# 47 further products on TensorE behind the last slot of a routed expert kernel

## The chip, the cores and the metric

One NeuronCore of a Trainium2 chip runs the whole kernel. The metric is the device time of one execution in microseconds (us). TensorE (PE) multiplies into PSUM banks, ScalarE (ACT) and VectorE (DVE) empty them, GpSimd (POOL) gathers and scatters rows by index, SyncE (SP) starts the other transfers.

## What is computed

Attention with a causal window of 64, a dense layer pair with a leaky activation, and a layer of eight experts, of which each token uses one. The last part is where the change stands:

```python
logits = x @ w_gate
expert_idx = np.argmax(logits, axis=1)
for e in range(E):
    mask = expert_idx == e
    xe = x[mask]
    h = np.maximum(xe @ w1[e], 0.0)
    ye = h @ w2[e]
    out[mask] = gate_w[mask, None] * ye
```

There are 2304 tokens, 512 features, 8 experts and 1024 hidden units.

## The kernel before, in words

Attention and the dense layers come first, in an order written out by hand (`PLAN`). Then the expert layer runs in slots. A slot is 128 tokens of one expert. The tokens of an expert rarely fill whole slots, so their number depends on the data: 20 slots (`SURE`) run always, and 5 more stand in nested conditional blocks, `tc.If(tot > s - K1)`, line 970. Each engine branches for itself. In the profiled execution slot 20 runs and the blocks of slots 21 to 24 are skipped (504 instructions of line 743 are 21 slots of 24).

Every value is split into a high and a low part in the type fp32r, and each product is done three times (high by high, low by high, high by low).

A slot (`slot`, line 914) does, in this order: `e1` (lines 715 to 717) multiplies the tokens by the first weights, 24 products of 128 rows, 128 outputs and 512 columns, into a bank of the tag `h`; `htr` (lines 726 to 730) turns the result on TensorE into a bank of the tag `att`, which ScalarE copies (line 729) and VectorE then reads a second time (line 730); `xtr` (lines 699 to 703) does the same for the next slot's tokens, with ScalarE at line 702 and VectorE at line 703; `e2mm` (line 743) multiplies by the second weights, 24 products, into `acc0` or `acc1`; `finish` scales (line 749) and scatters 128 rows to the output by an indirect transfer of GpSimd (line 750). Beside it `split2` makes the high part (ScalarE, line 819) and the low part (VectorE, line 825) of the next slot's weights, and `reload` (line 764) fetches those after them. All of it is issued in the order of the code (`tc.manual_schedule()`).

`pbank("att")` hands out three banks in turn, `pbank("h")` two. The split weights lie in 12 buffers `ring_t[4]` to `ring_t[15]`, used in turn; `xs[s]` holds the turned tokens of slot s, in one of two buffers. `pbank` hands out the bank that was used longest ago, so that the last to have read a bank is ScalarE and VectorE of some slot before.

An engine that skips a conditional block runs one event there, which adds to the engine's semaphore what the skipped instructions would have added, after its own last instruction (line 970 in the rows). So who waits for an instruction of a skipped block waits for that event. Behind the blocks stands the end of the program (line 1046 in the rows): SP waits for every transfer and every engine in turn, one event each, TensorE's count among the last three; then all engines drain and meet twice at a barrier that GpSimd leads.

Of the kernel before, what the change touches and what calls it, by code (L numbers as in the profile page):

```python
# [80 lines left out]
def attn_moe_moe_kernel(  # L81
# [11 lines left out]
    PE, ACT, DVE, POOL, SP = nc.tensor, nc.scalar, nc.vector, nc.gpsimd, nc.sync  # L93
# [131 lines left out]
    att = st1.enter_context(tc.tile_pool(name="att", bufs=1))  # L225
# [449 lines left out]
    xs = {}  # L675
# [79 lines left out]
    def sregs(s):  # L755
        p, r = where(s)
        ctl = tab["ctl", p]
        e = SP.value_load(ctl[0:1, 0, r:r + 1], min_val=0, max_val=NE - 1)
        ch = SP.value_load(ctl[0:1, 1, r:r + 1], min_val=0, max_val=1) if s else None
        regs[s] = (e, ch)  # L760

    def reload(s, t):
        e, ch = regs[s]
        SP.dma_start(out=raw2[t], in_=wx[bass.ds(e, 1), t].rearrange("o p c -> p (o c)"), cond=ch, cond_hint=False)
# [3 lines left out]
    ring_t = {}  # L768
# [145 lines left out]
    def slot(s):  # L914
        nx = s + 1 < NSLOT
        extra = {
            0: {0: [(r_trans, NB - 1, 0)], 1: [(r_trans, NB - 1, 1, "ht")], 2: [(r_logits, NB - 1, 0)],
                3: [(r_trans, NB - 1, 2), (r_logits, NB - 1, 1)], 4: [(r_logits, NB - 1, 2)], 7: [(r_gate, NB - 1)]},
            1: {1: [(r_rank, NB - 1), (r_place, NB - 1)], 6: [(r_onehot, NB - 1)]},
            2: {0: [(r_list, NB - 1), (r_add, NB - 1)], 1: [(r_onehot, NB - 1, 1)], 2: [(r_list, NB - 1, 1), (r_add, NB - 1)], 4: [(table_step,), (table_step,)]},  # L920
            3: {i: [(table_step,)] for i in (0, 2, 4, 6)},
        }.get(s, {})

        def step(i):
            for fn, *a in extra.get(i, []):
                fn(*a)
            if nx:
                split2(s + 1, i)
                if i % 2 and s + 2 < NSLOT:
                    if i == 1:  # L930
                        sregs(s + 2)
                    reload(s + 2, i // 2)

        e1(s, 0, 0)
        step(0)
        e1(s, 0, 1)
        step(1)
        e1(s, 1, 0)
        htr(s, 0)
        step(2)  # L940
        e1(s, 1, 1)
        step(3)
        e2mm(s, 0)
        htr(s, 1)
        step(4)
        if s + 2 < NSLOT:
            gather(s + 2)
        e2mm(s, 1)
        if nx:
            xtr(s + 1)  # L950
        step(5)
        e2mm(s, 2)
        step(6)
        e2mm(s, 3)
        finish(s)
        step(7)

    gen1 = slot_table(1)
    with tc.manual_schedule():
        sregs(1)  # L960
        for t in range(4):
            reload(1, t)
        for s in range(SURE):
            slot(s)
        tot = nc.values_load(tab["tot"][0:1, 0:1], min_val=0, max_val=NSLOT)
        st2 = ExitStack()
        for s in range(SURE, NSLOT):
            st2.enter_context(tc.If(tot > s - K1))
            slot(s)
        st2.close()  # L970


# [78 lines left out]
```

## Time and profile before

| | us |
|---|---|
| median of 2 runs | 768.01 (767.69 to 768.33) |
| the profiled execution, its own time | 768.02 |
| its span, first to last instruction | 766.2 |
| TensorE busy | 747.7 |
| VectorE busy | 609.1 |
| ScalarE busy | 456.3 |
| GpSimd busy | 89.0 |

The span is what the profile's rows cover; 1.8 us of the profiled execution lie outside it. A q behind an engine's name (PEldq, SPq) is its sequencer, which runs events, branches and drains. PEld is the loading of weights into TensorE, which has its own rows.

### The profile page before, as it was taken

How to read it: one execution, taken by the hardware profiler on the slowest of the kernel's cores; microseconds unless marked ns; L12 is line 12 of the kernel's file. 1: busy time of each engine (PE TensorE's matmuls, PEld its weight loads, DVE VectorE, ACT ScalarE, POOL GpSimd, SP SyncE). 2: the span in 40 equal slices, each digit the busy share in tenths (PEclk: the TensorE clock that was granted, in tenths of full speed). 3: DMA queues.
4: the chain of work that ended last, by engine and by line, in shares of the span. 5: the costliest groups of instructions: out<-in, count | busy, mean ns of one | idle time of the engine just before them, and what ended most of it. 6: DMA issues, size and time to landing. Idle time of an engine off the chain costs nothing.

```text
span 766.2 us, 12642 instructions
## 1 busy us (share of the span) xinstructions
PE 747.7 (98%) x4567; PEld 612.6 (80%) x4572; DVE 609.1 (79%) x1154; ACT 456.3 (60%) x868; POOL 89.0 (12%) x106
## 2 busy tenths in 40 slices
PE   7999999999999999999999999999999999999996
PEld 3688888788888888888888988777788888888884
DVE  4999999477556656668775956699999999999997
ACT  4887465533233333334342323778889898899986
POOL 1210001000000000000000001011222213131322
PEclk9999999999999999999999999999999999999998
DMA  9993423233033113122323116430195076766621
GB/s 343 412 367 131 147 74 117 70 86 122 18 100 97 62 57 103 62 97 90 92 69 111 56 42 250 168 119 28 56 340 182 29 270 265 284 236 248 212 75 51
DMA packets 29442, 109.90 MB, mean 143 GB/s; under 512 B 3582, under 2 KB 3966, under 8 KB 22208
## 3 DMA queue, kind: packets, MB, share of 16 engines
q1 hardware_dynamic: 25856, 98.25, 35.6%
q0 software_dynamic: 3520, 10.80, 4.2%
q8 instruction: 38, 0.62, 0.3%
q14 instruction: 28, 0.23, 0.1%
HBM read 154.09 MB, written 10.26 MB: 214 GB/s over the span
## 4 chain that ended last, share of the span: by engine, by line
PE 86%; DVE 8%; issue 2%; DMA 1%; ACT 1%; POOL 0%; SPq 0%; DVEq 0%
PE acc L743 12%; PE h L389 9%; PE acc L431 9%; PE acc L432 9%; PE h L390 8%; PE h L391 8%; PE acc L433 8%; DVE hl L825 4%; PE h L715 4%; PE h L717 4%; PE h L716 4%; PE att L364 2%; PE att L295 2%; PE att L341 2%; PE att L726 1%
## 5 line engine op out<-in xcount | busy, mean ns | idle before, releaser
L825 DVE TENSOR_TENSOR hl<-hl,hl 128x1024 fp32r<-128x1024 f32 x176 | 211.4, 1223 | 17.1 <-ACT hl L819 16.4
L819 ACT CAST hl<-hl 128x1024 fp32r<-128x1024 f32 x176 | 180.2, 1049 | 4.6 <-DMA hl<-in_wx_dram 3.4
L743 PE MATMUL acc<-hl,xl 128*128 128x512 f32 x504 | 130.7, 400 | 2.4 <-DVE xl L730 2.3
L404 ACT ACTIVATE g<-h 128x512 f32<-128x512 f32 (+1 forms) x80 | 44.6, 557 | 142.6 <-PE h L391 112.3
L389 PE MATMUL h<-xh,hl 128*128 128x512 f32 (+1 forms) x320 | 120.5, 377 | 0.7 <-DVE g L408 0.7
L390 PE MATMUL h<-xl,hl 128*128 128x512 f32 (+1 forms) x320 | 118.1, 369 | 0.0
L391 PE MATMUL h<-xh,hl 128*128 128x512 f32 (+1 forms) x320 | 118.0, 369 | 0.0
L432 PE MATMUL acc<-hl,gl 128*128 128x512 f32 x288 | 113.2, 393 | 0.4 <-DVE gl L414 0.4
L433 PE MATMUL acc<-hl,gh 128*128 128x512 f32 x288 | 112.6, 391 | 0.0
L431 PE MATMUL acc<-hl,gh 128*128 128x512 f32 x288 | 109.9, 400 | 0.0
L743 PEld LDWEIGHTS acc<-hl,xl 128*128 128x128 f32 x504 | 91.2, 188 | 21.3 <-DVE xl L730 3.7
L408 DVE SCALAR_TENSOR_TENSOR g<-g,beta,h 128x512 f32<-128x512 f32 (+1 forms) x80 | 55.3, 691 | 56.1 <-ACT g L404 55.9
L414 DVE TENSOR_TENSOR gl<-g,gh 128x512 fp32r<-128x512 f32 (+1 forms) x80 | 50.8, 635 | 38.4 <-PE acc L432 24.1
L349 ACT CAST gh<-g 128x512 fp32r<-128x512 f32 (+1 forms) x80 | 46.5, 581 | 51.4 <-DVE g L408 49.7
L691 POOL DMA_INDIRECT gx<-x1d,ixg x23 | 39.9, 1736 | 290.5 <-DVE xh L703 167.1
L389 PEld LDWEIGHTS h<-xh,hl 128*128 128x128 f32 x320 | 60.1, 188 | 10.9 <-issue 1.2
L715 PE MATMUL h<-hl,xh 128*128 128x512 f32 x168 | 67.7, 403 | 0.0
L485 DVE SCALAR_TENSOR_TENSOR dot<-stage,wge 128x512 bf16<-128x512 f32 x96 | 65.9, 686 | 1.8 <-DMA wge<-in_wgt_dram 0.4
L390 PEld LDWEIGHTS h<-xl,hl 128*128 128x128 f32 x320 | 60.1, 188 | 8.5 <-DVE xl L377 0.5
L717 PE MATMUL h<-hl,xh 128*128 128x512 f32 x168 | 66.1, 393 | 0.3 <-DVE xh L703 0.2
L391 PEld LDWEIGHTS h<-xh,hl 128*128 128x128 f32 x320 | 60.1, 188 | 7.9
L716 PE MATMUL h<-hl,xh 128*128 128x512 f32 x168 | 65.5, 390 | 0.0
(194 smaller groups left out, 1070.8 us busy)
## 6 DMA issues: line engine op xcount, KB each, us to landing
hl<-in_wx_dram SPq DMA_DIRECT2D x92, 1024.0 KB
hl<-in_wcat_dram SPq DMA_DIRECT2D x14, 1024.0 KB
qk<-in_qkv_dram SPq DMA_DIRECT2D x30, 448.0 KB
v<-in_qkv_dram SPq DMA_DIRECT2D x30, 256.0 KB
wge<-in_wgt_dram SPq DMA_DIRECT2D x24, 256.0 KB
x1d<-stage SPq DMA_DIRECT2D x3, 1032.0 KB
hl<-in_qkv_dram SPq DMA_DIRECT2D x6, 448.0 KB
x<-in_wcat_dram SPq DMA_DIRECT2D x2, 1024.0 KB
```

Of the source, the lines that this page charges most:

```text
L389: PE.matmul(out=h[:, 0:n], lhsT=w_in_op(f, k, 0), rhs=xh[:, k, :], start=(k == 0), stop=False)
L390: PE.matmul(out=h[:, 0:n], lhsT=w_in_op(f, k, 0), rhs=xl[:, k, :], start=False, stop=False)
L391: PE.matmul(out=h[:, 0:n], lhsT=w_in_op(f, k, 1), rhs=xh[:, k, :], start=False, stop=(k == 3))
L431: PE.matmul(out=a, lhsT=gh[:, c0:c0 + 128], rhs=w_out_op(f, 0), start=(f == 0), stop=False)
L432: PE.matmul(out=a, lhsT=gl[:, c0:c0 + 128], rhs=w_out_op(f, 0), start=False, stop=False)
L433: PE.matmul(out=a, lhsT=gh[:, c0:c0 + 128], rhs=w_out_op(f, 1), start=False, stop=(f == 15))
L715: PE.matmul(out=o, lhsT=th[:, k, :], rhs=wh, start=(k == 0), stop=False)
L716: PE.matmul(out=o, lhsT=th[:, k, :], rhs=wl, start=False, stop=False)
L717: PE.matmul(out=o, lhsT=tl[:, k, :], rhs=wh, start=False, stop=(k == 3))
L743: PE.matmul(out=o, lhsT=x[:, f % 4, :], rhs=w[:, lo, (f % 2) * 512:(f % 2) * 512 + 512], start=(x is th and f == 0 and lo == 0), stop=(x i ...
L819: ACT.copy(out=t[:, 0, :], in_=r)
L825: eng.tensor_tensor(out=t[:, 1, :], in0=r, in1=f32(t[:, 0, :]), op=ALU.subtract)
```

## The change

Behind the conditional blocks, outside all of them, TensorE runs 47 products. Their stationary operand is a part of `xs[0][0]`, the moving one a part of the high half of `ring_t[4]`, and they write the three `att` banks and one `h` bank, each with `start=True`; nobody reads the banks afterwards. In order: 5 of the usual shape; 12 of 64 rows, by turns the upper and the lower half, by turns into two banks; 16 of 32 rows, the four quarters by turns into four banks; 6 with 256 columns; 4 with 64 outputs; 4 of 64 rows, all the upper half and one bank. Nothing else changes.

```diff
+    def probe():
+        x, y = xs[0][0], ring_t[4][:, 0, 0:512]
+        b = [pbank("att") for _ in range(3)] + [pbank("h")]
+
+        def mm(o, r0, r1, m=128, n=512):
+            PE.matmul(out=o[0:m, 0:n], lhsT=x[r0:r1, 0, 0:m], rhs=y[r0:r1, 0:n], start=True, stop=True)
+
+        for _ in range(5):
+            mm(b[0], 0, 128)
+        for i in range(12):
+            mm(b[i % 2], 64 * (i % 2), 64 * (i % 2) + 64)
+        for i in range(16):
+            mm(b[i % 4], 32 * (i % 4), 32 * (i % 4) + 32)
+        for _ in range(6):
+            mm(b[0], 0, 128, 128, 256)
+        for _ in range(4):
+            mm(b[0], 0, 128, 64)
+        for _ in range(4):
+            mm(b[0], 0, 64)
+
...
         st2.close()
+        probe()
```

## Rows read from the trace of the kernel before

**Rows 1.** The page: span, TensorE's busy time, the clock in 40 slices

```profile
span 766.2 us, 12642 instructions
...
PE 747.7 (98%) x4567; PEld 612.6 (80%) x4572; DVE 609.1 (79%) x1154; ACT 456.3 (60%) x868; POOL 89.0 (12%) x106
...
PEclk9999999999999999999999999999999999999998
```

**Rows 2.** Timeline of 757 to 767 us: start us, us, engine, line, operation

```profile
756.77 2.00 PE L743 MATMUL acc<-hl,xl 128*128 128x512 f32 x8
...
758.10 3.63 DVE L825 TENSOR_TENSOR hl<-hl,hl 128x1024 fp32r<-128x1024 f32 x3
...
759.39 1.04 ACT L819 CAST hl<-hl 128x1024 fp32r<-128x1024 f32 x1
760.47 1.02 POOL L750 DMA_INDIRECT out_dram<-gx,ixs  x1 [0.30 <-ACTq L970]
```

**Rows 3.** Line 970, 755 to 767 us: ns min/median/max, first and last start

```profile
L970 PEldq COMPARE_BRANCH  x2: 200/1766/3332, 755.9 to 759.5; - x2
...
L970 PEldq EVENT_SEMAPHORE  x1: 51/51/51, 759.3 to 759.3; - x1
...
L970 ACTq EVENT_SEMAPHORE  x1: 17/17/17, 760.5 to 760.5; - x1
L970 DVEq EVENT_SEMAPHORE  x1: 21/21/21, 761.8 to 761.8; - x1
```

**Rows 4.** Line 1046, the end of the program, whole span

```profile
L1046 POOLq EVENT_SEMAPHORE  x4: 17/17/17, 765.4 to 766.1; - x4
L1046 POOLq DRAIN  x3: 46/113/4170, 761.2 to 766.0; - x3
L1046 SPq DRAIN  x3: 7/7/13, 764.3 to 765.7; - x3
L1046 PEldq DRAIN  x2: 8/8/8, 759.8 to 765.7; - x2
```

**Rows 5.** Line 1046 in 763 to 764.4 us

```profile
L1046 SPq EVENT_SEMAPHORE  x12: 27/28/336, 763.2 to 764.2; - x12
```

**Rows 6.** The chain that ended last, 735 to 767 us: start us, us, what

```profile
743.24 0.44 PE att L699 x4
743.67 2.75 PE acc L743 x12
```

**Rows 7.** Timeline of TensorE, 62 to 66 us, where the shape changes twice

```profile
62.94 0.39 PE L391 MATMUL h<-xh,hl 128*128 128x512 f32 x1
63.26 1.10 PE L295 MATMUL att<-qk 64*64 64x128 f32 x32
64.29 0.50 PE L431 MATMUL acc<-hl,gh 128*128 128x512 f32 x1
64.63 0.40 PE L432 MATMUL acc<-hl,gl 128*128 128x512 f32 x1
64.87 0.40 PE L433 MATMUL acc<-hl,gh 128*128 128x512 f32 x1
```

**Rows 8.** Timeline of TensorE, 7 to 12.9 us

```profile
7.90 1.99 PE L295 MATMUL acc<-qk 64*64 64x128 f32 x32 [2.72 <-DMA qk<-in_qkv_dram]
9.81 1.04 PE L271 MATMUL att<-c 128*128 128x512 bf16 x2
10.64 0.91 PE L286 MATMUL acc<-c 128*128 128x512 bf16 x2
```

**Rows 9.** Stretches of the start and the end: us, busy (count), granted clock, DMA

```profile
8.00:10.00 2.00, 2.00 (x33) 1.61 (x34) 0.07 (x1) 0.00 (x0) 0.00 (x0) 0.50 1.09 423
10.00:12.00 2.00, 2.00 (x24) 0.82 (x26) 1.69 (x6) 0.40 (x3) 0.25 (x1) 0.68 0.97 402
758.00:762.00 4.00, 0.76 (x4) 0.30 (x2) 3.72 (x4) 2.13 (x3) 2.90 (x2) 1.00 0.19 56
762.00:763.00 1.00, 0.00 (x0) 0.00 (x0) 0.00 (x0) 0.00 (x0) 0.00 (x0) 0.60 0.53 195
763.00:766.20 3.20, 0.00 (x0) 0.00 (x0) 0.00 (x0) 0.00 (x0) 0.00 (x0) 0.50 0.00 0
```

**Rows 10.** Timeline, 746 to 747.5 us: weight loads beside products

```profile
746.49 0.39 PE L716 MATMUL h<-hl,xh 128*128 128x512 f32 x1
746.49 0.19 PEld L717 LDWEIGHTS h<-hl,xh 128*128 128x128 f32 x1
...
746.72 0.39 PE L717 MATMUL h<-hl,xh 128*128 128x512 f32 x1
```

## The prediction

> **What bounds the kernel now.** I read the page first: TensorE is busy 747.7 of 766.2 us at the full clock [rows 1], so over the whole span it is the bound, and a product put in the middle would cost its full time. But the change stands behind the last slot, so I read the last 10 us. In the timeline TensorE's last product ends at 756.77 + 2.00 = 758.77, ScalarE's last copy at 760.43, VectorE's last subtraction at 758.10 + 3.63 = 761.73, GpSimd's scatter at 761.49 [rows 2]. From 758.77 to the span's end, 7.4 us, TensorE does nothing. What ends last there is none of the working engines. The lines of the end show that SP has gone through its waits by 764.3, and that the longest of GpSimd's three drains takes 4.17 us from 761.2, to 765.4; only then does GpSimd's first barrier event come, and 0.8 us later the span ends [rows 4]. So the path at the end is GpSimd's drain, and TensorE has slack: its own last count is asked for by SP among its last three events, about 764.2 [rows 5], and up to about 0.2 us before 765.4 it could come without harm.
>
> **When the products can start.** TensorE leaves the blocks early: its event there is at 759.3 and its drain at the end at 759.8 [rows 3, 4]. The products need their operands (written by ScalarE) and their banks free. The first bank, the one used longest ago, was last read by VectorE, by the low half of an `xtr` in a block that is skipped; what stands for it is VectorE's event at line 970, at 761.8, behind its last subtraction [rows 2, 3]. ScalarE's event, at 760.5, is earlier. So the change adds a wait on TensorE until 761.8. Queued behind it are the other 46 products and TensorE's drain, and for that drain and count SP and the barrier wait. First weight load about 761.85.
>
> **What the 47 products take.** Between products of the usual shape the chain has 2.75 us for 12, a step of 0.229 us; the 0.39 us of one row is latency, not step [rows 6, 10]. Part by part, at the full clock:
>
> 5 usual: 5 x 0.229 = 1.15.
>
> 12 of half the rows: attention runs 32 products of 64 x 64 in 1.10 us at the full clock [rows 7], 0.87 us without the last one's latency of about 0.23, thus 0.11 for four. A turn at 128 x 128 with the same 128 columns steps by 0.44/4 = 0.11 too [rows 6]. So four quarter-arrays run beside each other at the price of one product. Those are halves of rows crossed with halves of outputs; I take from it that the two row halves run as a pair: 6 x 0.229 = 1.37. The bound from the other side is 12 x 0.229 = 2.75, if fp32r in halves doesn't pair.
>
> 16 of a quarter: no row shows 32 rows. By the same reading four run together, 4 x 0.229 = 0.92; one by one 16 x 0.229 = 3.66. I take 0.92, by the nearest row, attention's four at once. [...]
>
> 6 with 256 columns: between 0.11 (the turn) and 0.229; half the columns of the usual shape, so 0.12, 0.72 in all, at most 1.37.
>
> 4 with 64 outputs and 4 on one half: the columns set the step, and nothing alternates, 8 x 0.229 = 1.83. If the 64 outputs were cheaper it would be at least half of that.
>
> Together 1.15 + 1.37 + 0.92 + 0.72 + 1.83 = 5.99. The shape changes five times. At a change before, the first product of the new shape starts 63.26 - 62.94 = 0.32 us behind the last of the old one, 0.09 over the step, and the second comes 64.63 - 64.29 = 0.34 behind the first, 0.11 over [rows 7]. That makes 0.2 a change, 1.0 in all; the start from standing costs the second part once more, 0.1; the last product's latency beyond its step is 0.39 - 0.23 = 0.16. Sum 7.25 us: 761.85 + 7.25 = 769.1.
>
> [...]
>
> **The clock.** [...] At the start of the kernel it was 0.50 from 7.9, when products began, and the mean of 0.68 over 10 to 12 puts the rise at 10 + 2 x 0.32/0.5 = 11.3 [rows 8, 9], so 3.4 us of low clock with TensorE at work. At the low clock the step is longer: 10.64 - 9.81 for two, 0.415, for bf16, and 1.99 against 1.10 us for attention's 32 [rows 7, 8], about 1.85 times. So 3.4 us at half speed do the work of 1.7 and cost 1.7: end at 770.8. If the clock stays up, 769.1.
>
> **The end.** From TensorE's end SP still needs two events (0.06 each: 11 steps from about 763.55 to 764.2) and its drains, 0.2 with the signal [rows 4, 5]; GpSimd's drain has long ended, so the barrier follows at once and takes the same 0.8. With 0.1 for the signals: 770.8 + 1.1 = 771.9 for the span, 5.7 over 766.2. Outside the span lie 1.8 us before (768.02 - 766.2), and I leave them: 773.7. The profiled 768.02 is the median, so no correction. No other engine, queue or transfer gets an instruction, and everything up to 758.77 is as it was; its cost I put at nothing, with no bound that the rows suggest. What is late next is TensorE itself, with GpSimd's drain under it, 5 us early. [...]
>
> **The rivals.**
> *An early start.* TensorE doesn't wait for VectorE's event and starts at 759.85, at the full clock. End 759.85 + 7.25 = 767.1, span 768.2, time 770.0. Against it: VectorE reads each `att` bank second. 7 in 100.
> *No pairs.* Row halves and quarters run one by one: 1.37 + 2.74 = 4.1 more, 777.8. For it: no row of fp32r in parts of the rows. Against: attention's four at once. 12 in 100.
> *The clock stays low* to the end, since parts of the array keep it there: 7.25 x 1.85 = 13.4 us in place of 7.25 + 1.7 = 8.95, so 778.2. Against it: attention's parts at 7.9 were followed by the rise [rows 8, 9]. 9 in 100.
> [...] 3 in 100.
> *The other side, slower by over 2%.* One mechanism: parts of rows neither pair nor count as work for the clock, so that all 47 go one by one at the low clock: (41 x 0.229 + 0.72 + 1.26) x 1.85 = 21.0 us (1.26 for changes of shape, start and latency), end 782.9, time 785.8. It decides from 783.4, 2% over. 3 in 100.
> *Nothing to see.* The products end before 765.2 and GpSimd's drain hides them, 768.0: this needs the early start and a sum of 5.3 instead of 7.25. 3 in 100.
>
> **How the numbers follow.** The forecast, start at VectorE's event, pairs and fours, has 63 in 100; with the clock up all the time it gives 772.0, with a start or signals 1 us later some 775. Its own range is 771.5 to 775. To hold 8 in 10 I take in the early start at 770.0 and the two cases at 778; the 785.8 and the 768.0 stay out. Range 769.8 to 778.4. Faster or slower by over 2% (about what a measurement of this kernel can tell from no change) means below 752.7 or above 783.4. Only the other side is there: slower 0.03, faster 0.005 for what I can't name, same 0.965.
>
> **What would show it.** In the changed profile: the rows of the slots unchanged; TensorE's first new product at 761.8 to 762.0, right behind VectorE's event; the 12 halves in about 1.4 us at the full clock, two starting together; the 16 quarters in 0.9, four together; a gap of 0.3 at each change of shape; the clock at 0.50 for some 3.4 us from about 762.2; GpSimd's drain still ending at 765.4 with SP's last events now at TensorE's end; span 770 to 772. It is wrong if TensorE starts before 761, if the halves step by 0.23 each, or if something ahead of 758 moved.

## The result, and the profile after

The kernel with the change takes 772.63 us, the median of two executions (772.15 and 773.12), against 768.01 before: a ratio of 1.0059, with an interval of 1.0043 to 1.0075. That is 4.6 us more, below the 2% that a measurement of this kernel can tell in general; the interval still excludes no change at all. The forecast was 773.7, with 772.0 for a clock that stays up. The profiled execution is the one of 772.15, and in it the clock stayed up.

The page of the changed kernel: the span, the engines' busy time, and the clock in 40 slices.

```profile
span 770.4 us, 12737 instructions
PE 756.3 (98%) x4614; PEld 617.8 (80%) x4619; DVE 609.1 (79%) x1154; ACT 456.1 (59%) x868; POOL 89.0 (12%) x106
PEclk9999999999999999999999999999999999999999
```

Beside [rows 1], the other engines' busy time is where it was and TensorE has more. The span is 4.2 us longer and 1.75 us lie outside it, as before. The end of the timeline (start us, us, engine, line, operation; the probe's products stand at L963, and what was line 970 is L990):

```profile
758.48 3.62 DVE L825 TENSOR_TENSOR hl<-hl,hl 128x1024 fp32r<-128x1024 f32 x3
...
762.31 1.80 PE L963 MATMUL att<-hl,xh 128*128 128x512 f32 x6 [3.16 <-DVEq L990]
...
763.95 0.39 PE L963 MATMUL att<-hl,xh 64*128 64x512 f32 x1
763.95 0.39 PE L963 MATMUL acc<-hl,xh 64*128 64x512 f32 x1
764.18 0.39 PE L963 MATMUL att<-hl,xh 64*128 64x512 f32 x1
764.19 0.39 PE L963 MATMUL acc<-hl,xh 64*128 64x512 f32 x1
...
764.88 0.39 PE L963 MATMUL acc<-hl,xh 64*128 64x512 f32 x1
765.20 0.49 PE L963 MATMUL att<-hl,xh 32*128 32x512 f32 x1
765.21 0.50 PE L963 MATMUL acc<-hl,xh 32*128 32x512 f32 x1
765.21 0.49 PE L963 MATMUL att<-hl,xh 32*128 32x512 f32 x1
765.21 0.49 PE L963 MATMUL h<-hl,xh 32*128 32x512 f32 x1
765.54 0.40 PE L963 MATMUL att<-hl,xh 32*128 32x512 f32 x2
...
767.03 0.73 PE L963 MATMUL att<-hl,xh 128*128 128x256 f32 x3
...
767.15 0.84 PE L963 MATMUL att<-hl,xh 128*64 128x512 f32 x3
...
768.72 0.62 PE L963 MATMUL att<-hl,xh 64*128 64x512 f32 x2
```

The halves start two at a time within 10 ns, the quarters four at a time, and the next pair or four comes 0.23 us or so behind (763.95, 764.18; a first four at 765.20, a second at 765.54 with the change of shape in it). Here a pair or a four costs what one product costs, 0.23. The last product ends at 768.72 + 0.62 = 769.34. The two merged rows at 767 show the one change of shape that costs nothing: the last product of 256 columns starts at 767.03 and the first with 64 outputs at 767.15, the step of 0.12 that 256 columns have. The end of that second row agrees: 767.15, two steps of 0.23 and the latency of 0.39 make 768.0, where the row ends at 767.99.

The events of line 990, from 755 to 771 us (ns min/median/max, first and last start), answer to [rows 3]:

```profile
L990 PEldq EVENT_SEMAPHORE  x1: 51/51/51, 760.0 to 760.0; - x1
...
L990 ACTq EVENT_SEMAPHORE  x1: 17/17/17, 760.8 to 760.8; - x1
L990 DVEq EVENT_SEMAPHORE  x1: 21/21/21, 762.1 to 762.1; - x1
```

TensorE is there at 760.0, ScalarE's event comes at 760.8, and the first product starts at 762.31, behind VectorE's event at 762.1. The end of the program (was line 1046) answers to [rows 4]:

```profile
L1067 SPq EVENT_SEMAPHORE  x14: 17/28/4977, 763.6 to 770.3; - x14
L1067 POOLq EVENT_SEMAPHORE  x4: 17/17/17, 769.6 to 770.3; - x4
L1067 POOLq DRAIN  x3: 46/112/4030, 761.6 to 770.1; - x3
```

GpSimd's long drain now takes 4.03 us from 761.6, until 765.6, but its first barrier event comes only at 769.6: the barrier waits for SP, whose longest event, 4.98 us, is the wait for TensorE, by the list of what SP waited for:

```profile
SPq L1067 <- PE att L963: 5.0, 1, 5.0
```

The path at the end has passed from GpSimd's drain to TensorE. The stretches (us; busy and count of PE, PEld, DVE, ACT, POOL; granted clock; DMA share; GB/s) show the clock:

```profile
762.00:763.00 1.00, 0.69 (x3) 0.64 (x4) 0.10 (x1) 0.00 (x0) 0.00 (x0) 1.00 0.79 270
763.00:770.40 7.40, 6.34 (x46) 3.83 (x44) 0.00 (x0) 0.00 (x0) 0.00 (x0) 1.00 0.01 2
```

Where [rows 9] fell to 0.60 and then 0.50, this execution has 1.00 to the end.

### The profile page after: what moved, and what is told of

Same layout as the page of the kernel before. It is cut to its first block, busy times and chain, and to the rows that moved or that the text cites. A ratio compares the mean times of both kernels' runs of the same rounds, so it can differ in the third digit from the quotient of the medians.

```text
span 770.4 us, 12737 instructions
## 1 busy us (share of the span) xinstructions
PE 756.3 (98%) x4614; PEld 617.8 (80%) x4619; DVE 609.1 (79%) x1154; ACT 456.1 (59%) x868; POOL 89.0 (12%) x106
```

## The experiments

Ratios are to the kernel before, run beside each on the same chip; in brackets stands the interval, behind the median the lowest and highest time. The kernel before took 768.84 (766.57 to 770.19) beside the first four, 767.98 beside the next four, 768.2 beside the last.

### The change once more

No edit.

> The change as it is, more often. Mine: the time has two levels that differ by whether the clock falls while TensorE waits for VectorE: about 772.1 with the clock at 1.00 to the end (as profiled), about 1 to 1.7 more with a low stretch. The rival, that the spread of the two executions (772.15 and 773.12) is the usual one of this kernel: then the kernel before, run beside it, spreads as widely, and the low clock does not go with the longer times.

773.76 us (773.26 to 774.58), ratio 1.0065 [1.0052, 1.0078]. The forecast of 773.7 was for a clock that falls, and here it fell. Stretches of the profiled execution, same columns as above:

```profile
763.00:764.00 1.00, 0.83 (x3) 0.72 (x4) 0.00 (x0) 0.00 (x0) 0.00 (x0) 0.78 0.66 224
764.00:767.00 3.00, 3.00 (x12) 1.98 (x12) 0.00 (x0) 0.00 (x0) 0.00 (x0) 0.50 0.01 3
767.00:768.00 1.00, 1.00 (x14) 0.55 (x16) 0.00 (x0) 0.00 (x0) 0.00 (x0) 1.00 0.00 0
```

A mean of 0.78 puts the fall to 0.50 at 0.44 us before 764, at 763.56; the rise is at 767, so 3.4 us low. TensorE had stood still for 3.17 us and begun again 0.4 us before the fall. The products show both levels:

```profile
763.17 0.47 PE L963 MATMUL att<-hl,xh 128*128 128x512 f32 x1 [3.17 <-DVEq L990]
...
765.82 0.62 PE L963 MATMUL att<-hl,xh 64*128 64x512 f32 x1
765.83 0.62 PE L963 MATMUL acc<-hl,xh 64*128 64x512 f32 x1
766.25 0.62 PE L963 MATMUL att<-hl,xh 64*128 64x512 f32 x1
...
770.58 1.19 PE L963 MATMUL att<-hl,xh 64*128 64x512 f32 x4
```

At a clock of 0.50 a pair steps 0.43 us (765.82 to 766.25) in place of 0.23. From first start to last end the 47 take 771.77 - 763.17 = 8.60 us here and 769.34 - 762.31 = 7.03 in the first profile: the fall costs 1.57 us. All five executions have a mean clock of 0.996, as the slower of the first two had (773.12), and the other of those 1.000 (772.15). Such a mean also holds a low stretch near the start of the kernel, where there is one: from 7.9 to 11.3 us in the kernel before [rows 9], from 9.2 to 12.6 here (a clock of 0.81 in 8 to 10 us, 0.50 in 10 to 12, 0.84 in 12 to 14), none in the first profile. But 0.996 stands for some 6 us of low clock (an estimate, 0.004 x 774 / 0.5), more than one stretch of 3.4. The spread of the kernel before, 3.6 us over 18 executions, is wide enough to hold such differences, so the times alone would not show the price; the two profiles do.

### Other banks: ScalarE's event in place of VectorE's

```diff
-        b = [pbank("att") for _ in range(3)] + [pbank("h")]
+        b = [pbank("acc0"), pbank("acc1"), pbank("h"), pbank("h")]
```

> The 47 products write the banks acc0, acc1 and both h, which ScalarE alone read last. Mine: they start at ScalarE's event, 1.3 us ahead of VectorE's, and all behind them moves with it: 1.3 less than the change, about 770.8, the clock up in nearly every execution since TensorE stands still for 1.8 us only. The rival, that the branch and the fetch of the new instructions set the start: no earlier start, 772.1 to 773.

770.84 us (769.45 to 771.55), ratio 1.0030 [1.0019, 1.0042]. Events of line 990 in it:

```profile
L990 ACTq EVENT_SEMAPHORE  x1: 17/17/17, 759.5 to 759.5; - x1
L990 DVEq EVENT_SEMAPHORE  x1: 21/21/21, 760.8 to 760.8; - x1
```

Its first product starts at 759.57, behind ScalarE's event and 1.2 us ahead of VectorE's, and the clock stays at 1.00. The median comes out 2.9 us below that of the change run beside it, and two terms add up to this: 1.3 between the two events and 1.57 for a fall that TensorE, after 1.76 us of standing still, doesn't meet in this profile. (Three of the six executions have a mean clock of 1.000. Three have 0.998: by 0.002 x 771 / 0.5, an estimate, some 3 us of low clock, and where it lay was not seen.) So the wait that sets the start of the change is the bank's last reader, not the operands or TensorE's own path, and it was worth both the start and, in the profile, the clock. Whether the start here hangs on the banks or on the operands, which ScalarE wrote as well, this run doesn't tell: both stand behind the same event.

### The first five products alone

The other five loops are left out.

> Only the five usual products of the 47 are left. Mine: TensorE ends at about 763.9, before SP asks for it at 764.4 and before GpSimd's drain ends at 765.6, so they are hidden: within 0.4 us of the kernel before. The rival, that work behind the blocks has a price of its own (fetch, semaphores, a later barrier): at least 1.3 more than before.

767.95 us (766.56 to 769.37, 12 executions), ratio 0.9994 [0.9984, 1.0004]. The end of the program in it:

```profile
L1057 POOLq EVENT_SEMAPHORE  x4: 17/17/17, 765.0 to 765.7; - x4
L1057 POOLq DRAIN  x3: 46/112/4531, 760.4 to 765.5; - x3
```

Its products end at 761.68 + 1.19 = 762.87, the drain at 760.4 + 4.53 = 764.9, and the barrier comes with the drain. What TensorE did by then cost nothing: a ratio of 0.9994.

### All parts of one height on the same rows

```diff
-            mm(b[i % 2], 64 * (i % 2), 64 * (i % 2) + 64)
+            mm(b[i % 2], 0, 64)
...
-            mm(b[i % 4], 32 * (i % 4), 32 * (i % 4) + 32)
+            mm(b[i % 4], 0, 32)
```

> The 12 halves all use the upper half of the rows and the 16 quarters the first quarter, with the banks by turns as before: the same count and shapes, no two row groups beside each other. Mine: each steps by 0.23, so 6 x 0.23 + 12 x 0.23 = 4.1 more than the change, about 776.3. The rival, that products on parts of the rows are cheap by themselves, whichever rows: no more than the change, 772 to 773.

783.78 us (782.52 to 786.04), ratio 1.0196 [1.0179, 1.0212]: 10.0 over the change beside it, where 18 further steps of 0.23 are 4.1. The expectation of 776.3 had no price for the clock. Stretches:

```profile
765.00:770.00 5.00, 5.00 (x12) 3.66 (x12) 0.00 (x0) 0.00 (x0) 0.00 (x0) 0.50 0.00 0
770.00:778.00 8.00, 8.00 (x19) 5.28 (x18) 0.00 (x0) 0.00 (x0) 0.00 (x0) 0.50 0.00 0
778.00:783.00 5.00, 5.00 (x14) 3.15 (x14) 0.00 (x0) 0.00 (x0) 0.00 (x0) 0.50 0.00 0
```

The clock fell at the start (a mean of 0.53 over 762 to 765 puts the fall at 762.2, where TensorE's first product starts at 762.94), and then it never came back in this profile, though TensorE was busy without a break from 762.94 to 783.24. All five executions have a mean clock of 0.984 to 0.988. The products ran one by one at 0.43 us, 20.3 us in all with the other shapes (762.94 to 783.24). The forecast's rival for the other side had 21.0 us for just this: neither pairs nor a clock that comes back.

### The same, started early

The last edit and the banks of the second experiment together: parts one by one, but from a clock that is up.

> As the run with one row group, but into the banks acc0, acc1 and h, so that TensorE starts at ScalarE's event, with the clock still up. Mine, since the low clock there lasted from the wait to the end of the program: single products on a part of the rows neither raise the clock nor hold it. Then the clock starts at 1.00 and falls while the halves or quarters run, and the time lies between 6.2 and 13 us over the kernel before. The rival, that the clock was low only for the wait ahead and then stuck: it stays at 1.00 to the end, 2.0 + 4.1 = 6.1 over before.

778.32 us (776.94 to 778.52), ratio 1.0129 [1.0113, 1.0144]. Stretches, and one row of the timeline:

```profile
761.00:767.00 6.00, 5.88 (x24) 4.29 (x25) 1.32 (x2) 0.02 (x1) 1.02 (x1) 1.00 0.21 66
767.00:768.00 1.00, 1.00 (x6) 0.77 (x5) 0.00 (x0) 0.00 (x0) 0.00 (x0) 0.85 0.00 0
768.00:774.00 6.00, 6.00 (x18) 3.79 (x16) 0.00 (x0) 0.00 (x0) 0.00 (x0) 0.50 0.00 0
774.00:775.00 1.00, 1.00 (x4) 0.78 (x4) 0.00 (x0) 0.00 (x0) 0.00 (x0) 0.73 0.00 0
```

```profile
762.82 1.54 PE L963 MATMUL acc<-hl,xh 64*128 64x512 f32 x6
```

Six halves on the same rows take (1.54 - 0.39) / 5 = 0.23 us a step at the full clock: no pairs, and each load hidden behind the product ahead of it. From 762.8 to 765.1 the products are busy for all 2.30 us and ten loads, of 0.18 each, for 1.84 of them. The clock fell at about 767.7, in the middle of the quarters, with no pause of TensorE since 761.1, and rose at about 774.5, when the products of full height had run again. Together the products take 14.25 us (761.12 to 775.37): 7.03, 4.1 for the missing pairs, and 3.1 for 6.8 us of low clock. All four executions have a mean clock of 0.995 or 0.996. So parts run one by one neither brought the clock back (the experiment before, 0.50 to the end) nor kept it up (0.50 from 767.7).

### All 47 of the usual shape

All six loops are replaced by `for _ in range(47): mm(b[0], 0, 128)`.

> All 47 products of the usual shape, 128 rows and 512 columns, in the banks and at the start of the change. Mine: the low stretch lasts about 3.4 us as in the change, and then the clock rises, for full products follow: 47 x 0.229 + 0.16 + 0.1 = 11.0 in place of 7.04, and the same 1.6 for the clock: 4.9 + 4.0 = 8.9 over before. The rival, that the clock once low stays low behind the blocks whatever runs: 47 x 0.427 = 20 us, some 16 over before.

777.40 us (775.81 to 777.86), ratio 1.0115 [1.0098, 1.0131]. That is 9.4 over the kernel before, where 8.9 was expected. In its profile the clock fell and came back within 3.4 us, as in the change run again; the products take 774.96 - 762.44 = 12.52, which is 46 x 0.229 + 0.39 + 0.1 = 11.0 and the 1.5 of the fall. The execution whose clock was 1.000 throughout took 775.81. So 47 steps, 12.52 us, are far more than the 8.60 that the change run again pays with a fall of the same length: its parts do run beside each other.

### More changes of shape, the same number of steps

```diff
-        for i in range(12):
-            mm(b[i % 2], 64 * (i % 2), 64 * (i % 2) + 64)
-        for i in range(16):
-            mm(b[i % 4], 32 * (i % 4), 32 * (i % 4) + 32)
+        for j in "HHQHQHQHQH":
+            p = 2 if j == "H" else 4
+            for i in range(p):
+                mm(b[i], 128 // p * i, 128 // p * (i + 1))
```

> The same products, but pairs of halves and fours of quarters by turns (H H Q H Q H Q H Q H, six pairs and four fours), 7 more changes of shape. Mine: 0.2 a change at the full clock, 1.4 over the change, up to 2 where the clock is low: 6.3 to 6.9 over before. The rival, that a change of shape costs nothing and the 0.3 steps of the rows are the latency of what ran before: 4.9 over before, as the change.

777.67 us (773.56 to 777.98), ratio 1.0116 [1.0096, 1.0136]; the expectation was missed in the times. The profiled execution is the one of 773.56, with the clock at 1.00:

```profile
764.27 0.49 PE L963 MATMUL h<-hl,xh 32*128 32x512 f32 x1
764.69 0.50 PE L963 MATMUL att<-hl,xh 64*128 64x512 f32 x1
764.70 0.50 PE L963 MATMUL acc<-hl,xh 64*128 64x512 f32 x1
765.12 0.50 PE L963 MATMUL att<-hl,xh 32*128 32x512 f32 x1
```

Every step is 0.43 here (764.26, 764.69, 765.12), 0.20 over the usual 0.23. The products take 770.74 - 762.29 = 8.45 us, 1.42 more than in the change for seven further changes of shape: 0.20 each, as expected. What was missed is the clock: three of the five executions lie some 4 us higher, with a mean clock of 0.991; by 0.009 x 776 / 0.5, an estimate, their clock was low for some 14 us, where the change run again shows 0.996 and 6.8 us (3.4 at the start of the kernel, 3.4 here). None of the three was profiled, so where it was low was not seen.

### A later start

```diff
+        for _ in range(4):
+            DVE.memset(b[0], 0.0)
```

Four memsets of VectorE on the first bank, ahead of the products.

> VectorE writes zeros into the first bank four times before the 47 products, so that TensorE stands still for some 2.4 us longer and the clock is certain to be low at the start. Mine: the low clock costs at most the same as in the change, since it rises after some 3.4 us of products: 4.9 + 2.4 = 7.3 over before, a little more where the change itself had started ahead of the fall. The rival, that a longer stand costs a longer low stretch: 9 or more over before.

776.34 us (776.05 to 777.52), ratio 1.0113 [1.0097, 1.0128]: 8.4 over the kernel before, between the two expectations. Timeline and stretches:

```profile
762.95 0.48 DVE L962 MEMSET att<- 128x512 f32 x1 [0.18 <-DVE att L962]
...
763.58 0.77 PE L965 MATMUL att<-hl,xh 128*128 128x512 f32 x1 [6.14 <-DVE att L962]
```

```profile
762.00:763.00 1.00, 0.00 (x0) 0.00 (x0) 0.64 (x3) 0.00 (x0) 0.00 (x0) 0.79 0.00 0
763.00:769.00 6.00, 5.42 (x21) 3.47 (x21) 0.43 (x1) 0.00 (x0) 0.00 (x0) 0.50 0.00 0
769.00:770.00 1.00, 1.00 (x16) 0.72 (x16) 0.00 (x0) 0.00 (x0) 0.00 (x0) 0.80 0.00 0
```

A memset takes 0.48 us and the next starts 0.67 behind it, so the first product comes 3.15 us behind VectorE's event at 760.43, 2.9 later than in the change. The clock fell before TensorE began and stayed low from 762.6 to 769.4, 6.8 us, twice as long as in the change run again. The products took 773.23 - 763.58 = 9.65 us, 1.05 more than in the change run again. So by the profile the later start adds its 2.9 and the longer low stretch another 1.05, beside a rise of 3.4 in the medians (8.36 for 4.92). The first expectation, a low stretch of the same length, missed; the longer stretch is that of its rival, though the time stayed under the 9 that the rival had. Whether the longer stand made it longer is not shown: the early start with parts one by one, further up, had 6.8 us too, with no stand of TensorE for 6.6 us ahead of its fall.

### The first 33 products, started early

The banks of the second experiment, with only the usual products, the halves and the quarters.

> The first 33 of the 47 products (5 usual, 12 halves, 16 quarters) into the banks that ScalarE read last. Mine: started at ScalarE's event they end some 4.2 us behind it, 0.7 us before GpSimd's drain, and cost nothing: within 0.4 us of the kernel before. The rival, that the five products alone were hidden because they were few, and that SP's wait for TensorE or the fetch of more instructions shows with 33: 1 us or more over before.

768.59 us (768.02 to 769.28, 11 executions), ratio 1.0005 [0.9996, 1.0014]. Its last quarters, and GpSimd's drain:

```profile
764.63 0.39 PE L963 MATMUL h<-hl,xh 32*128 32x512 f32 x2
```

```profile
L1061 POOLq DRAIN  x3: 46/113/4371, 761.6 to 766.5; - x3
```

The products end near 765.0, the drain at 761.6 + 4.37 = 766.0. Thirty-three of the 47 products cost nothing when they start 1.3 us earlier. No version that ran is faster than the kernel before; this one and the one with five products equal it.

## Why the prediction was right

**What bounds the end.** Right. GpSimd's drain set the end before; products that end ahead of it cost nothing (five alone, a ratio of 0.9994; thirty-three early, 1.0005), and those that end behind it move the end one for one: in the eight profiles where they do, the span ends 1.03 to 1.07 us behind the last product.

**The start.** The cause was right: VectorE's event, as the other banks show. The size was off by 0.42 us: the first load was put at 761.85 and came at 762.27, the first product at 762.31. Of that, 0.37 is VectorE, whose last subtraction ended at 758.48 + 3.62 = 762.10 in this execution and at 761.73 in [rows 2]; the change gives VectorE nothing to do, and the spans of the kernel before scatter over more than that. The rest is the way from event to load. The forecast had named "something ahead of 758 moved" as a sign of being wrong; these 0.37 are such a move, and the scatter is the only account of it here.

**The products.** 7.25 forecast from first load to last end, 7.07 measured (762.27 to 769.34). Pairs and fours were right: 0.23 a pair (763.95, 764.18), and 0.235 a four (from 765.54 to the last four at 766.01 in two steps). The one term off is that of the shape changes, "five times ... 0.2 a change, 1.0 in all": only four of the five cost, 0.2 each, as the mixed order shows once more. From 256 columns to 64 outputs, both of full height, there was no price: a step of 0.12 (767.03 to 767.15). With four changes the forecast's sum is 7.05.

**The clock.** Forecast: it falls at about 762.2, just behind the first products, stays low 3.4 us, costs 1.7. The 762.2 was an estimate from the kernel before, where the mean of 0.60 over 762 to 763 puts the fall [rows 9]. In the change run again the clock did so, 3.4 us, at a price of 1.57. The 1.7 was taken at half speed; by the forecast's own factor of 1.85 it would be 3.4 x (1 - 1/1.85) = 1.56. (Both readings behind that factor give 1.81; the steps measured here, 0.43 and 0.23, give 1.87.) In the profile after, the clock did not fall. So the same kernel came out with the fall, 0.4 us behind its first product, and without it, where the forecast chose the fall. The time from TensorE's stop to the fall was not one value: 3.4 us in the kernel before (758.77 to 762.2), 5.1 with the later start (757.44 to 762.6). The forecast named both sums, 773.7 and 772.0; the measured 773.76 and 772.15 lie at these. That 772.0 was met is in part luck, errors that cancel: 0.42 for the start, against 0.2 for the fifth change of shape and less than 0.1 at the end. That 773.7 was met is luck in part as well: the kernel before took 768.84 beside that run and 768.01 beside the first, so the change with the fall cost 4.9 us, where the forecast had 5.7.

**The end.** 1.1 from TensorE's end to the span's, forecast; 770.4 - 769.34 = 1.1 measured. Right.

**The rivals.** The early start, forecast at 2.0 us over the kernel before, is what the other banks make, and it measures 2.0. The equal number is partly luck: there TensorE waits for ScalarE's event, 1.3 us ahead of VectorE's, where the rival waited for nothing and started 2.0 ahead. No pairs: against it stands the profile after, with 0.23 a pair and 0.235 a four. And loads on the same rows hid behind the products in the early start with single parts: six halves stepped 0.23 with loads of 0.18. A clock that stays low to the end: not in the change (1.00 from 767 on in the run with the fall), but in the kernel with all parts on the same rows (0.50 to 784.3). The other side's mechanism, parts that neither pair nor count for the clock, is half real: with pairs taken away by hand both halves of it come true, at 14.9 us over the kernel before, where the forecast had 17.8. It was kept out by the pairs, since the order of the change puts neighbours on different rows.

## What to carry to other kernels

Ask first what ends last: here, products on an idle TensorE behind the last slot were free as long as they ended ahead of GpSimd's drain (33 of them, a ratio of 1.0005), and where they ended behind it the span ended 1.03 to 1.07 us behind the last of them. Which bank such work wrote decided here when it could start: the first product stood behind VectorE's event with the `att` banks (762.1 and 762.31) and behind ScalarE's with the others (759.5 and 759.57), and that choice alone was worth 2.9 of 4.9 us. In these runs products on part of the rows cost a half or a quarter (0.23 us for two or four) only where neighbours in the order used different rows (here also different banks); the same products on the same rows cost full steps, 0.23 us each at a clock of 1.00 and 0.43 at 0.50, and in the two profiles with all parts on the same rows the clock stood at 0.50 for 22 us (762.2 to the end) and for 6.8.

## What was not expected of the hardware

The clock fell while TensorE was busy without a break: in the early start with all parts on the same rows it went from 1.00 to 0.50 at 767.7, 6.6 us after the products began, and where they started as late as in the change, it stayed at 0.50 for their last 18 us, with no break either (765 to 783.24).

The low stretch comes in more than one length: 3.4 us in the change run again, 6.8 with the later start and with single parts started early. The mixed order's three slower executions had more low clock in all than the change, by their means. What decides between the lengths stays open.

A change of shape cost 0.20 us of TensorE wherever the height of the products changed (128, 64 and 32 rows, in the orders that ran), and nothing in the one place where only columns and outputs changed (a step of 0.12, 767.03 to 767.15).

What GpSimd's drain of 4.0 to 4.5 us waits for, and whether quarters on different rows also run beside each other when they write one bank, wasn't tried.
